# Attention and a feed-forward layer on one core: weight preparation at the lowest rank, x written in one piece, two steps of each block held back

## The chip, the cores and the metric

The kernel runs on one core of a Trainium2 chip. The metric is the device time of one execution in microseconds (us), the median of three runs. The kernel is written against a tile framework: the program is emitted by Python code, and a scheduler sets at build time in which order the instructions stand on each engine.

## The reference

Softmax attention with a learned relative-position bias, followed by a feed-forward layer with a hard-swish-like gate:

```python
scores = (q @ k.transpose(0, 1, 3, 2)) / sqrt(D)          # B=4, H=8, S=576, D=64
x = (log1p(|i - j|) / log1p(max(i, 1)))[..., None]
bias = relu(x @ w1 + b1) @ w2                             # hidden 32, one value per head
attn = softmax(scores + bias)                             # over the keys
y = attn @ v                                              # to [B*S = 2304 tokens, 512]
h = y @ w_in                                              # 512 x 2048
g = h * clip(h + 3, 0, 6) / 6
out = g @ w_out                                           # 2048 x 512
```

The feed-forward weights arrive as 64-bit floats.

## The kernel before

**Units and tiles.** The attention is cut into 32 units (b, p, u): a batch b, one of four pairs of heads p, and a part u of the query rows. Part u=0 has 256 query rows (four tiles t = 0 to 3, each 128 rows of one pair), part u=1 has 320 (five tiles t = 4 to 8; tile 8 holds the last 64 rows of both heads). That makes 144 tiles. The loop over n walks them: `front(n)` issues QK of tile n+1 (PE, `s_ps`, L560 or L540), the softmax's first pass on DVE (`bt`, `sm`, L572), the division into a high and a low fp16 part (`hl`: ACT L129, DVE L146), three tiles later the transposing DMA from SP's queue (`at<-hl`, L648), and at a unit's end PV (PE, `pv_ps`, L719, 28 matmuls). `back(n)` writes x, that is the attention output scaled and split into fp16 high (ACT, L733) and low (DVE, L146) parts, and runs the exponential (ACT, L583). The units with b < 2 and u=0 take a "direct" fp32 path instead (`t_ps`, `atf`, L631, L673).

**Feed-forward blocks.** When all four pairs of a (b, u) are through, its x is a block of 256 or 320 tokens, and `ffn(b, u)` is put on a queue. It is a generator of 32 steps of 12 matmuls: 16 h-steps (`h_ps`, L794, contracting over all 512 columns of x, each followed by ACT, DVE, ACT and POOL work on the result: L784, L777, L771, L773) and 16 o-steps (`o_ps`, L817). The loop takes about 1.55 to 2 such steps for each tile, by a credit. From tile 37 on (`steady`), PE executes in the order in which the code emits: a matmul that must wait holds up everything behind it on PE. Four PSUM banks are shared by `h_ps`, `o_ps`, `pv_ps` and the bias's `b_ps`.

**Weights.** `w_in_prep` and `w_out_prep` (generators `gen_w` and `gen_o`) load each weight in eight pieces, rebuild it on ACT, POOL and DVE (L258 to L272), take its largest value, and bring that to one number over all partitions through a small transpose on PE (`m_ps`, L159; then `p_w` L161 and a row of small DVE instructions that ends in `r_w1c` or `r_w2c`, L222), by which the rows are scaled. `r_w2c` also scales the first block's g (L127), and only then can the first o_ps begin. The scheduler picks among ready instructions by a rank; the generators run through `low`, which shifts the rank by `CFG['pw']` and `CFG['po']` (both 0 before). `CFG['os']` is the number of w_out steps after which they are taken at a faster rate.

The bias tensor is computed on the way (`z_e`, `b_ps`, `bo`), written to memory and read back by tile (`bt<-bias`).

Of the kernel before, what the change touches and what calls it, by code (L numbers as in the profile page):

```python
# [29 lines left out]
CFG = {'z0': 'AD', 'gz': 12, 'z1': 'AD', 'gz2': 16, 'zeng': 'DDA', 'sg': 'P', 'wm1': 'A', 'wm2': 'RRAAAAAA', 'hl': 'A', 'gl': 'PP', 'vm': 'A', 'g0': 8, 'rwi': 2.0, 'rw0': 0.3, 'rw1': 0.7, 'ro': 0.85, 'rb': 1.7, 'rf0': 1.3, 'rf': 2.0, 'rf1': 1.55, 'la': 6, 'gq': 2, 'gap': 0.0, 'wu': 8, 'act': 'o', 'g1': 2, 'w64': 5, 'rfo': 2.3, 'tv': 'A', 'pw': 0, 'po': 0, 'gr': 'AD', 'wb': 3, 'fb': 2, 'spn': 45, 'sw': 37, 'ws': 2, 'kn': 10, 'kw': 1, 'os': 11, 'ro2': 2.0, 'bo': 12, 'rb0': 1.5, 'psw': 21, 'xp': 0, 'mw': 2, 'he': 0}  # L30
# [5 lines left out]
def attention_moe_kernel(  # L36
# [227 lines left out]
    def f64_pack(lo, sign, u, top):  # L264
        ub = u.bitcast(U32)
        nc.vector.tensor_scalar(
            out=u, in0=u, scalar1=F64_MAX, scalar2=0.0, op0=ALU.min, op1=ALU.max, accum_out=top,
        )
        nc.vector.scalar_tensor_tensor(
            out=ub, in0=ub, scalar=3, in1=sign, op0=ALU.logical_shift_left, op1=ALU.bitwise_or  # L270
        )
        nc.vector.scalar_tensor_tensor(  # L272
            out=ub, in0=lo, scalar=29, in1=ub, op0=ALU.logical_shift_right, op1=ALU.bitwise_or
        )
# [9 lines left out]
    def w_in_prep():  # L284
# [19 lines left out]
        def pack(k, tu):  # L304
            f64_pack(*tu, parts[:, k:k + 1])
            if k % 2:
                c = k // 2
                nc.vector.tensor_reduce(
                    out=top[:, c:c + 1], in_=parts[:, k - 1:k + 1], op=ALU.max, axis=AX.X
                )  # L310
                row_scale(top[:, c:c + 1], pw[:, c:c + 1], sw[:, c:c + 1])
# [196 lines left out]
    COLS = [0, 256, 128, 384, 0, 384, 128, 512, 256]  # L508
# [102 lines left out]
    def direct(b, p, t):  # L611
        return b < cfg["fb"] and t < 4

    def unit_tile(n):
# [8 lines left out]
        return at_t[b, p, u][:, :, COLS[t]:COLS[t] + 128]  # L623
# [22 lines left out]
    def soft_turn(n):  # L646
        if not direct(*tiles[n]):
            nc.sync.dma_start_transpose(out=unit_tile(n), in_=a_t.pop(n))  # L648

    XPARTS = [  # L650
        [(slice(0, 128), 0, 256, 0)],
        [
            (slice(0, 64), 0, 320, 0),
            (slice(64, 128), 0, 64, 256),
            (slice(64, 128), 64, 320, 0),
        ],
    ]
# [69 lines left out]
    def x_high(b, p, u):  # L727
        if direct(b, p, 4 * u):
            return x_first(b, p)
        ps = pv_t[b, p, u]  # L730
        x = x_tile(b, u)
        for rows, lo, hi, tok in XPARTS[u]:
            nc.scalar.activation(  # L733
                out=x[rows, 0, p, tok:tok + hi - lo], in_=ps[rows, lo:hi], func=AF.Copy,
                scale=pscale["x"][rows, p:p + 1],
            )

    def x_low(b, p, u):
# [4 lines left out]
        for rows, lo, hi, tok in XPARTS[u]:  # L743
            low_part(
                x[rows, 1, p, tok:tok + hi - lo], ps[rows, lo:hi],
                pscale["x"][rows, p:p + 1], x[rows, 0, p, tok:tok + hi - lo],
            )
# [398 lines left out]
    START, SWITCH = 21, cfg["sw"]  # L1146
    in_order = ctx.enter_context(ExitStack())
# [46 lines left out]
    out_steps = [0]  # L1194

# [6 lines left out]
    def ffn_step():  # L1202
        nonlocal phase
        r = next(queue[0], "end")
        if r == "w2":
            phase = 1.5
        if r == "end":
            queue.pop(0)
            phase = 2
# [10 lines left out]
    for n in range(-1, NT + 7):  # L1220
# [22 lines left out]
        if queue:  # L1243
# [4 lines left out]
            while credit >= 1.0 and queue and (phase < 2 or steady[0] or cfg["he"]):  # L1248
# [69 lines left out]
```

## Time and profile before

| | us |
|---|---|
| median of 3 runs | 681.77 (680.17 to 683.64) |
| the profiled execution | 680.92 |
| its span | 679.1 |
| PE busy | 631.2 |
| ACT busy | 519.8 |
| DVE busy | 478.9 |

The profiled execution is read from its first to its last instruction (the span). The execution's own time has 1.8 us around the span. A busy time is the sum of the stretches in which an engine had an instruction under way, not the time at which it works at its peak.

### The profile page before, as it was taken

Reading aid. Unit: us, or ns where it says so; the run is one execution under the profiler, and the core shown is the slowest. Engines: PE = TensorE matmul, PEld = TensorE weight load, DVE = VectorE, ACT = ScalarE, POOL = GpSimd, SP = SyncE. Lnnn points to the kernel's source line nnn. Section 1 sums busy time; section 2 is a strip of 40 time slices with the busy share of each in tenths; the row PEclk is TensorE's granted clock in tenths of the full one; section 3 lists DMA queues with packets and bytes.
Section 4 is the critical chain, followed back from the end, with each engine's and each line's share of the span. In section 5 each row is a group of like instructions: output and inputs, shape, how many; then the busy total and the mean of one; then the engine's idle time right before and its main releaser. Section 6 shows DMA issues by size and latency. Waiting matters only on the chain. (4 is left out here: it accounts for less than half of the span.)

```text
span 679.1 us, 14803 instructions
## 1 busy us (share of the span) xinstructions
PE 631.2 (93%) x5424; PEld 449.8 (66%) x5424; DVE 478.9 (71%) x1150; ACT 519.8 (77%) x1032; POOL 210.6 (31%) x267
## 2 busy tenths in 40 slices
PE   7677889787998999999999999999999999999997
PEld 2224546555676767688887786767776777777775
DVE  7889977999737887777688777777777768811310
ACT  7986877887939997998699878987799779922620
POOL 1111115855102441154134413541244313310420
PEclk9997999997999999999999999999999999999999
DMA  8899768571768979979999899979977796420000
GB/s 295 297 339 339 296 246 317 184 271 57 192 182 208 236 191 283 217 217 203 280 278 232 175 202 195 190 148 181 206 178 150 166 197 126 98 60 20 1 11 29
DMA packets 176136, 130.56 MB, mean 192 GB/s; under 512 B 137792, under 2 KB 145216, under 8 KB 175040
## 3 DMA queue, kind: packets, MB, share of 16 engines
q1 hardware_dynamic: 166272, 114.14, 67.5%
q10 hardware_dynamic: 9792, 15.49, 7.1%
q8 instruction: 42, 0.69, 0.4%
q14 instruction: 30, 0.25, 0.1%
HBM read 77.54 MB, written 15.49 MB: 137 GB/s over the span
## 5 line engine op out<-in xcount | busy, mean ns | idle before, releaser
L794 PE MATMUL h_ps<-x,wi 128*128 128x256 f16 (+1 forms) x1536 | 199.7, 287 | 8.3 <-DVE t L777 4.0
L817 PE MATMUL o_ps<-g,wo 128*128 128x256 f16 (+1 forms) x1536 | 195.8, 286 | 0.3 <-DVE t L777 0.3
L794 PEld LDWEIGHTS <-wi 128*128 128x128 f16 x1536 | 147.2, 98 | 56.5 <-issue 14.4
L817 PEld LDWEIGHTS <-wo 128*128 128x128 f16 x1536 | 147.0, 98 | 47.0 <-issue 10.0
L773 POOL TENSOR_TENSOR g<-t,g 128x256 f16<-128x256 f32 (+1 forms) x128 | 101.6, 805 | 165.1 <-ACT g L771 155.4
L583 ACT ACTIVATE bt<-bt,sm 128x576 f32<-128x576 f32 x144 | 110.6, 769 | 43.6 <-DVE sm L572 41.2
L146 DVE SCALAR_TENSOR_TENSOR hl<-bt,sm,hl 128x576 f16<-128x576 f32 x112 | 93.9, 854 | 25.1 <-ACT hl L129 22.4
L419 POOL TENSOR_TENSOR qkl<-st,qkh 128x576 fp32r<-128x576 f32 (+2 forms) x48 | 56.4, 1196 | 98.3 <-ACT qkh L412 98.2
L129 ACT ACTIVATE hl<-bt,sm 128x576 f16<-128x576 f32 x112 | 83.9, 768 | 2.8 <-ACT bt L583 1.4
L777 DVE SCALAR_TENSOR_TENSOR t<-t,t,h_ps 128x320 f32<-128x320 f32 (+1 forms) x112 | 56.4, 515 | 37.0 <-ACT t L784 35.3
L572 DVE CUSTOM_DVE_ANT_0 bt<-s_ps,bt 128x576 f32<-128x576 f32 x88 | 64.7, 750 | 12.2 <-PE s_ps L560 5.7
L784 ACT ACTIVATE t<-h_ps,t,hr 128x320 f32<-128x320 f32 (+1 forms) x112 | 64.5, 588 | 4.4 <-PE h_ps L794 3.3
L771 ACT ACTIVATE g<-t 128x256 f16<-128x256 f32 (+1 forms) x128 | 55.0, 440 | 15.5 <-DVE t L777 14.8
L827 ACT ACTIVATE ot<-o_ps,os 128x256 f32<-128x256 f32 (+1 forms) x32 | 15.9, 496 | 52.7 <-PE o_ps L817 52.6
L591 DVE TENSOR_SCALAR sm<-sm 128x1 f32<-128x1 f32 x112 | 16.9, 151 | 42.9 <-ACT bt L583 42.7
L869 DVE TENSOR_SCALAR z_e<-T,nbp 128x576 f32<-128x576 f32 (+17 forms) x69 | 36.0, 568 | 4.3 <-PE b_ps L890 4.2
L929 ACT ACTIVATE bo<-b_ps,cv_sb,isc 128x576 f32<-128x576 f32 (+36 forms) x60 | 35.8, 636 | 2.5 <-PE b_ps L890 2.5
L146 DVE SCALAR_TENSOR_TENSOR x<-pv_ps,xr,x 64x320 f16<-64x320 f32 (+3 forms) x56 | 23.6, 445 | 18.1 <-ACT x L733 17.0
L873 ACT ACTIVATE z_e<-T,bp 128x576 f32<-128x576 f32 (+17 forms) x43 | 28.9, 694 | 9.7 <-PE b_ps L890 4.3
L631 PE MATMUL t_ps<-eye_sb,bt 128*128 128x128 f32 x160 | 26.3, 299 | 10.6 <-DVE sm L572 5.7
L631 PEld LDWEIGHTS t_ps<-eye_sb,bt 128*128 128x128 f32 x160 | 18.8, 150 | 20.9 <-ACT atf L634 7.8
L719 PE MATMUL pv_ps<-at,vh 128*64 128x320 f16 (+1 forms) x432 | 32.0, 293 | 0.3 <-DVE t L777 0.3
(127 smaller groups left out, 860.4 us busy)
## 6 DMA issues: line engine op xcount, KB each, us to landing
bt<-bias SPq DMA_DIRECT2D x36, 576.0 KB, 5.0
w<-in_w_in_dram SPq DMA_DIRECT2D x8, 1024.0 KB, 7.2
vs<-in_vp_dram SPq DMA_DIRECT2D x24, 320.0 KB, 4.4
st<-in_qk_dram SPq DMA_DIRECT2D x16, 448.0 KB, 4.6
bias<-bo ACTq DMA_DIRECT2D x20, 295.5 KB, 4.5
wo<-in_w_out_dram SPq DMA_DIRECT2D x5, 1024.0 KB, 5.9
bias<-bo ACTq DMA_DIRECT2D x16, 288.0 KB, 6.3
bt<-bias SPq DMA_DIRECT2D x32, 144.0 KB, 3.2
```

The costliest lines, as they stand in the source:

```text
L129: nc.scalar.activation(out=out, in_=full, func=AF.Copy, scale=scale)
L146: nc.vector.scalar_tensor_tensor(out=out, in0=full, scalar=scale, in1=high, op0=ALU.mult, op1=ALU.subtract)
L419: nc.gpsimd.tensor_sub(out=lo[:, c:c + w], in0=t[:, c:c + w], in1=hi[:, c:c + w].bitcast(F32))
L572: nc.vector.tensor_tensor_reduce(out=halves(bt), in0=ps, in1=halves(src), op0=ALU.add, op1=ALU.min, scale=-0.125, scalar=3.0e38, accum_out ...
L583: nc.scalar.activation(out=bt, in_=bt, func=AF.Exp, scale=-1.0, bias=sm[:, 0:1], accum_out=total)
L631: nc.tensor.transpose(tp[:, 128 * c:128 * c + 128], bt[:, j:j + 128], eye_sb)
L771: nc.scalar.activation(out=g[:, 0], in_=uu, func=AF.Copy)
L773: e.tensor_sub(out=g[:, 1], in0=uu, in1=g[:, 0])
L777: nc.vector.scalar_tensor_tensor(out=t_t[f], in0=t_t[f], scalar=cols(f)[2], in1=h_t.pop(f)[:, 0:n], op0=ALU.min, op1=ALU.mult,)
L784: nc.scalar.activation(out=t_t[f], in_=h_t[f][:, 0:n], func=AF.Relu, scale=cols(f)[0], bias=cols(f)[1],)
L794: nc.tensor.matmul(out=h_t[f][:, 0:n], lhsT=wi[:, a, c, f * 128:(f + 1) * 128], rhs=x[:, e, c], start=(k == 0), stop=(k == 3 * KC - 1),)
L817: nc.tensor.matmul(out=ops[:, 0:n], lhsT=wo[:, a, f, e * 128:(e + 1) * 128], rhs=g_t[f][:, r], start=(f == 0 and a == 0 and r == 0), stop= ...
```

## The change

In the table `CFG`, `pw` and `po` go from 0 to 1000, so that weight preparation ranks behind every other ready instruction, and `os` goes from 11 to 10. The rest is in the code:

- The packing of w_in chains its maximum through the accumulator's starting value instead of reducing two partial maxima (four small DVE instructions fewer).
- Tiles 5 and 7 go to other columns of the unit's transposed tile, and tile 8's transposing DMA is split into two of 64 rows, so that the columns of both heads' tokens lie together. x of a 320-token unit is then one 128x320 piece on ACT and one on DVE, where it was three each (64x320, 64x64, 64x256).
- In `steady`, when only one block is on the queue and 30 of its 32 steps are taken, its last two steps are kept back until the next block is queued (`held`), up to tile 149 (`LAST`). A block is queued one tile after PV of its last pair was issued and its x written.

```diff
@@ -261,10 +261,10 @@
         )
         return lo, hi.bitcast(U32), u
 
-    def f64_pack(lo, sign, u, top):
+    def f64_pack(lo, sign, u, top, first=0.0):
         ub = u.bitcast(U32)
         nc.vector.tensor_scalar(
-            out=u, in0=u, scalar1=F64_MAX, scalar2=0.0, op0=ALU.min, op1=ALU.max, accum_out=top,
+            out=u, in0=u, scalar1=F64_MAX, scalar2=first, op0=ALU.min, op1=ALU.max, accum_out=top,
         )
         nc.vector.scalar_tensor_tensor(
             out=ub, in0=ub, scalar=3, in1=sign, op0=ALU.logical_shift_left, op1=ALU.bitwise_or
@@ -302,12 +302,11 @@
             return f64_abs(t, stage[:, c, fs])
 
         def pack(k, tu):
-            f64_pack(*tu, parts[:, k:k + 1])
-            if k % 2:
-                c = k // 2
-                nc.vector.tensor_reduce(
-                    out=top[:, c:c + 1], in_=parts[:, k - 1:k + 1], op=ALU.max, axis=AX.X
-                )
+            c = k // 2
+            if k % 2 == 0:
+                f64_pack(*tu, parts[:, c:c + 1])
+            else:
+                f64_pack(*tu, top[:, c:c + 1], parts[:, c:c + 1])
                 row_scale(top[:, c:c + 1], pw[:, c:c + 1], sw[:, c:c + 1])
 
         def split(k, step):
@@ -505,7 +504,7 @@
         return out, src
 
     ORDER = [(0, 0), (0, 1), (1, 0), (1, 1), (2, 0), (2, 1), (3, 0), (3, 1), (4, 0)]
-    COLS = [0, 256, 128, 384, 0, 384, 128, 512, 256]
+    COLS = [0, 256, 128, 384, 0, 320, 128, 448, 256]
     UT = (range(4), range(4, 9))
     units = [(b, p, u) for u in range(2) for b in range(B) for p in range(PAIRS)]
     tiles = [(0, p, t) for ts in ((0, 1), (2, 3)) for p in range(2) for t in ts]
...
@@ -644,17 +647,16 @@
         a_t[n] = hl
 
     def soft_turn(n):
-        if not direct(*tiles[n]):
-            nc.sync.dma_start_transpose(out=unit_tile(n), in_=a_t.pop(n))
-
-    XPARTS = [
-        [(slice(0, 128), 0, 256, 0)],
-        [
-            (slice(0, 64), 0, 320, 0),
-            (slice(64, 128), 0, 64, 256),
-            (slice(64, 128), 64, 320, 0),
-        ],
-    ]
+        if direct(*tiles[n]):
+            return
+        hl = a_t.pop(n)
+        if tiles[n][2] < 8:
+            nc.sync.dma_start_transpose(out=unit_tile(n), in_=hl)
+            return
+        at = whole_unit(n)
+        for s in range(2):
+            c = 256 + QW[1] * s
+            nc.sync.dma_start_transpose(out=at[:, :, c:c + 64], in_=hl[64 * s:64 * s + 64])
 
     def x_tile(b, u):
         if (b, u) not in x_t:
@@ -729,22 +731,16 @@
             return x_first(b, p)
         ps = pv_t[b, p, u]
         x = x_tile(b, u)
-        for rows, lo, hi, tok in XPARTS[u]:
-            nc.scalar.activation(
-                out=x[rows, 0, p, tok:tok + hi - lo], in_=ps[rows, lo:hi], func=AF.Copy,
-                scale=pscale["x"][rows, p:p + 1],
-            )
+        nc.scalar.activation(
+            out=x[:, 0, p], in_=ps[:, 0:QW[u]], func=AF.Copy, scale=pscale["x"][:, p:p + 1]
+        )
 
     def x_low(b, p, u):
         if direct(b, p, 4 * u):
             return
         ps = pv_t.pop((b, p, u))
         x = x_tile(b, u)
-        for rows, lo, hi, tok in XPARTS[u]:
-            low_part(
-                x[rows, 1, p, tok:tok + hi - lo], ps[rows, lo:hi],
-                pscale["x"][rows, p:p + 1], x[rows, 0, p, tok:tok + hi - lo],
-            )
+        low_part(x[:, 1, p], ps[:, 0:QW[u]], pscale["x"][:, p:p + 1], x[:, 0, p])
 
     def ffn(b, u):
         x = x_t.pop((b, u))
@@ -1144,6 +1140,7 @@
     credit = 0.0
     out_ready = False
     START, SWITCH = 21, cfg["sw"]
+    HOLD, LAST = 2, NT + 5
     in_order = ctx.enter_context(ExitStack())
 
     def keep_order(*names):
@@ -1192,6 +1189,10 @@
         keep_order("PE")
 
     out_steps = [0]
+    taken = [0]
+
+    def held():
+        return steady[0] and len(queue) == 1 and n < LAST and taken[0] >= 32 - HOLD
 
     def out_step():
         if next(gen_o, "end") == "end":
@@ -1201,11 +1202,13 @@
 
     def ffn_step():
         nonlocal phase
+        taken[0] += 1
         r = next(queue[0], "end")
         if r == "w2":
             phase = 1.5
         if r == "end":
             queue.pop(0)
+            taken[0] = 0
             phase = 2
         return r != "end" and r != "w2"
 
@@ -1245,7 +1248,7 @@
                 credit = cfg["gap"]
             else:
                 credit += cfg["rf0"] if phase == 1 else cfg["rfo"] if phase < 2 else cfg["rf1" if unit_no[min(n, NT - 1)] >= 16 else "rf"]
-            while credit >= 1.0 and queue and (phase < 2 or steady[0] or cfg["he"]):
+            while credit >= 1.0 and queue and (phase < 2 or steady[0] or cfg["he"]) and not held():
                 if ffn_step():
                     credit -= 1.0
                 if phase == 1.5 and not out_ready:
```

What the change moves, as the scheduler puts it.

SP's queue at the start of the program, before (`w` are pieces of w_in, `qk` and `vf` operands of the direct path):

```order
L248 DMA w_181<-in_w_in_dram 128x2048
L248 DMA w_185<-in_w_in_dram 128x2048
L395 DMA qk_219<-in_qkd_dram 128x1088
L395 DMA qk_237<-in_qkd_dram 128x1088
L395 DMA qk_255<-in_qkd_dram 128x1088
L395 DMA qk_280<-in_qkd_dram 128x1088
L179 DMA vf<-in_vp_dram 128x640
L248 DMA w_262<-in_w_in_dram 128x2048
```

The same place after the change:

```order
L394 DMA qk_219<-in_qkd_dram 128x1088
L394 DMA qk_237<-in_qkd_dram 128x1088
L394 DMA qk_255<-in_qkd_dram 128x1088
L394 DMA qk_280<-in_qkd_dram 128x1088
L179 DMA vf<-in_vp_dram 128x640
L248 DMA w_181<-in_w_in_dram 128x2048
L248 DMA w_185<-in_w_in_dram 128x2048
L248 DMA w_262<-in_w_in_dram 128x2048
```

The first two pieces of w_in moved behind the five loads of the direct path.

DVE at the second weight reduction, from the reduced maximum `p_w` to `r_w2c`, before:

```order
L146 SCALAR_TENSOR_TENSOR wo<-cu,w2s,wo 128x1024
L161 TENSOR_REDUCE p_w_1698<-m_ps 128x1
L146 SCALAR_TENSOR_TENSOR hl<-bt,sm,hl 128x576
L220 RECIPROCAL rm_w_1700<-p_w_1698 128x1
L203 TENSOR_SCALAR os_1761<-hs_992,p_w_1698 128x1
L203 TENSOR_SCALAR os_2157<-hs_2153,p_w_1698 128x1
L203 TENSOR_SCALAR os_3351<-hs_3347,p_w_1698 128x1
L146 SCALAR_TENSOR_TENSOR hl<-bt,sm,hl 128x576
L222 TENSOR_SCALAR r_w2c<-w2p,rm_w_1700 128x8
```

And after the change:

```order
L152 TENSOR_REDUCE m_w_1690<-w2p 128x1
L594 RECIPROCAL sm<-sm 128x1 x2
L161 TENSOR_REDUCE p_w_1694<-m_ps 128x1
L203 TENSOR_SCALAR os_1770<-hs_988,p_w_1694 128x1
L203 TENSOR_SCALAR os_2166<-hs_2162,p_w_1694 128x1
L220 RECIPROCAL rm_w_1696<-p_w_1694 128x1
L203 TENSOR_SCALAR os_3366<-hs_3362,p_w_1694 128x1
L222 TENSOR_SCALAR r_w2c<-w2p,rm_w_1696 128x8
L146 SCALAR_TENSOR_TENSOR wo<-cu,w2s,wo 128x1024
```

The two `hl` (softmax's low parts) that stood between `p_w` and `r_w2c` stand behind it now, with seven of the g scalings ahead of them.

PE just ahead of the first o_ps, before (`s_ps` is QK, `t_ps` the direct path's transposes, the twelve h_ps matmuls of one step end in the first row here):

```order
L794 MATMUL h_ps<-x,wi 128x256
L560 MATMUL s_ps<-qkh 128x288 x2
L560 MATMUL s_ps<-qkl,qkh 128x288 x2
L560 MATMUL s_ps<-qkh,qkl 128x288 x2
L631 MATMUL t_ps<-eye_sb,bt 128x128 x5
L817 LDWEIGHTS wo
L817 MATMUL o_ps<-g,wo 128x256
L817 LDWEIGHTS wo
L817 MATMUL o_ps<-g,wo 128x256
L817 LDWEIGHTS wo
L817 MATMUL o_ps<-g,wo 128x256
```

And after the change, first the rows ahead of the same twelve h_ps (they begin in the last row):

```order
L634 MATMUL t_ps<-eye_sb,bt 128x128 x10
L559 MATMUL s_ps<-qkh 128x288 x2
L559 MATMUL s_ps<-qkl,qkh 128x288 x2
L559 MATMUL s_ps<-qkh,qkl 128x288 x2
L559 MATMUL s_ps<-qkh 128x288 x2
L559 MATMUL s_ps<-qkl,qkh 128x288 x2
L559 MATMUL s_ps<-qkh,qkl 128x288 x2
L159 MATMUL m_ps<-eye_sb,m_w_1690 128x128
L790 LDWEIGHTS wi
L790 MATMUL h_ps<-x,wi 128x256
```

then the rows behind them:

```order
L790 MATMUL h_ps<-x,wi 128x256
L886 MATMUL b_ps<-z_e,w_sb 32x320 x4
L813 LDWEIGHTS wo
L813 MATMUL o_ps<-g,wo 128x256
L813 LDWEIGHTS wo
L813 MATMUL o_ps<-g,wo 128x256
```

One more tile's three `s_ps` groups and the five `t_ps` used to stand between these h_ps and the first o_ps. The `s_ps` groups moved ahead of `m_ps`, the `t_ps` behind 45 of the o_ps matmuls. In the blocks from tile 37 on, PE's list after the change is one or two steps (12 or 24 matmuls) further along in each block than before. Where a block ends, PE's list had 36 o_ps matmuls of the old block behind the last pair's PV and now has 24, at the PV that ends at 337.84 us in the profile and at the one that ends at 401.62 us; right behind the 24 come h_ps matmuls of the new block.

## Rows read from the trace of the kernel before

**Rows 1.** The page: busy time by engine, and the chain that ended last, by line.

```profile
PE 631.2 (93%) x5424; PEld 449.8 (66%) x5424; DVE 478.9 (71%) x1150; ACT 519.8 (77%) x1032; POOL 210.6 (31%) x267
...
PE o_ps L817 16%; PE h_ps L794 12%; PE s_ps L560 3%; PE pv_ps L719 3%; DVE hl L146 1%; ACT hl L129 0%; ACT bt L583 0%; DVE x L146 0%; ACT t L784 0%; DMA bt<-bias 0%; DVE bt L572 0%; SPq L498 0%; ACT ot L827 0%; DVE t L777 0%; ACT vh L129 0%
```

**Rows 2.** Busy time by stage: start:end, length, busy us (instructions), PE clock, DMA share, GB/s.

```profile
0.00:160.00 160.00, 129.37 (x961) 72.27 (x961) 141.80 (x304) 129.49 (x218) 56.26 (x51) 0.98 0.76 276
160.00:172.50 12.50, 9.19 (x41) 6.93 (x42) 11.82 (x38) 7.86 (x15) 1.73 (x4) 0.59 0.35 85
172.50:205.00 32.50, 32.50 (x290) 23.85 (x288) 16.11 (x47) 21.46 (x44) 3.60 (x5) 1.00 0.71 192
205.00:245.00 40.00, 35.56 (x355) 25.88 (x354) 32.88 (x86) 39.04 (x85) 15.94 (x22) 1.00 0.86 200
245.00:515.00 270.00, 263.90 (x2495) 204.93 (x2493) 203.23 (x505) 230.37 (x487) 93.26 (x133) 1.00 0.96 212
```

**Rows 3.** Timeline of PE, 162 to 174 us: start, us, instruction, count, [idle before <-releaser].

```profile
162.52 1.33 PE L631 MATMUL t_ps<-eye_sb,bt 128*128 128x128 f32 x5 [3.87 <-DVE sm L572]
...
167.64 0.80 PE L159 MATMUL m_ps<-eye_sb,m_w 128*128 128x128 f32 x2
168.23 2.77 PE L794 MATMUL h_ps<-x,wi 128*128 128x256 f16 x12
...
172.56 0.49 PE L817 MATMUL o_ps<-g,wo 128*128 128x256 f16 x3
```

**Rows 4.** Timeline of DVE around the second p_w.

```profile
168.47 0.29 DVE L161 TENSOR_REDUCE p_w<-m_ps 128x1 f32<-128x128 f32 x1 [0.47 <-PE m_ps L159]
168.68 0.81 DVE L146 SCALAR_TENSOR_TENSOR hl<-bt,sm,hl 128x576 f16<-128x576 f32 x1
...
170.56 0.23 DVE L222 TENSOR_SCALAR r_w2c<-w2p,rm_w 128x8 f32<-128x8 f32 x1
```

**Rows 5.** Line 794: its matmuls, with first and last start; DVE's first p_w.

```profile
L794 PE MATMUL h_ps<-x,wi x1536: 269/299/422, 107.5 to 649.3; 128*128 128x256 f16 x96, 128*128 128x320 f16 x96
...
86.33 0.29 DVE L161 TENSOR_REDUCE p_w<-m_ps 128x1 f32<-128x128 f32 x1
```

**Rows 6.** Tile x: counts, duration ns min/median/max, span of starts, forms.

```profile
L733 ACT ACTIVATE x<-pv_ps,xr x56: 308/456/522, 220.4 to 612.8; 64x320 f16<-64x320 f32 x16, 64x64 f16<-64x64 f32 x16, 64x256 f16<-64x256 f32 x16, 128x256 f16<-128x256 f32 x8
L146 DVE SCALAR_TENSOR_TENSOR x<-pv_ps,xr,x x56: 290/486/545, 221.6 to 614.0; 64x320 f16<-64x320 f32 x16, 64x64 f16<-64x64 f32 x16, 64x256 f16<-64x256 f32 x16, 128x256 f16<-128x256 f32 x8
```

**Rows 7.** Timeline of DVE and PE at one x in three pieces.

```profile
356.62 1.25 DVE L146 SCALAR_TENSOR_TENSOR x<-pv_ps,xr,x 64x320 f16<-64x320 f32 x3
...
357.92 1.26 PE L794 MATMUL h_ps<-x,wi 128*128 128x256 f16 x10 [0.80 <-DVE x L146]
```

**Rows 8.** Waits of PE: us in total, times, longest.

```profile
PE h_ps L794 <- DVE x L146: 3.2, 4, 0.9
```

**Rows 9.** Timeline of PE and DVE where a block ends, 128x256 x.

```profile
337.84 4.10 PE L817 MATMUL o_ps<-g,wo 128*128 128x256 f16 x36
...
340.47 0.48 DVE L146 SCALAR_TENSOR_TENSOR x<-pv_ps,xr,x 128x256 f16<-128x256 f32 x1
```

**Rows 10.** The next block's end, 128x320 x: PE, then ACT, then DVE.

```profile
401.62 4.11 PE L817 MATMUL o_ps<-g,wo 128*128 128x256 f16 x36
...
405.18 1.19 ACT L733 ACTIVATE x<-pv_ps,xr 64x320 f16<-64x320 f32 x3
...
405.45 0.81 DVE L146 SCALAR_TENSOR_TENSOR hl<-bt,sm,hl 128x576 f16<-128x576 f32 x1
406.40 1.25 DVE L146 SCALAR_TENSOR_TENSOR x<-pv_ps,xr,x 64x320 f16<-64x320 f32 x3
```

**Rows 11.** SP: the transposes (count, ns min/median/max, starts), and its waits.

```profile
L648 SPq DMA_TRANSPOSE at<-hl x112: 1242/1332/2941, 169.5 to 597.5; - x112
...
DMA to landing us min/median/max: 3.2/4.4/8.8
...
SPq L648 <- DVE hl L146: 48.7, 26, 7.6
```

More of the change, by code (lines that the diff above doesn't have):

```diff
@@ L29 @@
 VC = 5 * 128
-CFG = {'z0': 'AD', 'gz': 12, 'z1': 'AD', 'gz2': 16, 'zeng': 'DDA', 'sg': 'P', 'wm1': 'A', 'wm2': 'RRAAAAAA', 'hl': 'A', 'gl': 'PP', 'vm': 'A', 'g0': 8, 'rwi': 2.0, 'rw0': 0.3, 'rw1': 0.7, 'ro': 0.85, 'rb': 1.7, 'rf0': 1.3, 'rf': 2.0, 'rf1': 1.55, 'la': 6, 'gq': 2, 'gap': 0.0, 'wu': 8, 'act': 'o', 'g1': 2, 'w64': 5, 'rfo': 2.3, 'tv': 'A', 'pw': 0, 'po': 0, 'gr': 'AD', 'wb': 3, 'fb': 2, 'spn': 45, 'sw': 37, 'ws': 2, 'kn': 10, 'kw': 1, 'os': 11, 'ro2': 2.0, 'bo': 12, 'rb0': 1.5, 'psw': 21, 'xp': 0, 'mw': 2, 'he': 0}
+CFG = {'z0': 'AD', 'gz': 12, 'z1': 'AD', 'gz2': 16, 'zeng': 'DDA', 'sg': 'P', 'wm1': 'A', 'wm2': 'RRAAAAAA', 'hl': 'A', 'gl': 'PP', 'vm': 'A', 'g0': 8, 'rwi': 2.0, 'rw0': 0.3, 'rw1': 0.7, 'ro': 0.85, 'rb': 1.7, 'rf0': 1.3, 'rf': 2.0, 'rf1': 1.55, 'la': 6, 'gq': 2, 'gap': 0.0, 'wu': 8, 'act': 'o', 'g1': 2, 'w64': 5, 'rfo': 2.3, 'tv': 'A', 'pw': 1000, 'po': 1000, 'gr': 'AD', 'wb': 3, 'fb': 2, 'spn': 45, 'sw': 37, 'ws': 2, 'kn': 10, 'kw': 1, 'os': 10, 'ro2': 2.0, 'bo': 12, 'rb0': 1.5, 'psw': 21, 'xp': 0, 'mw': 2, 'he': 0}
 F64_BIAS = 2.0 ** -112
@@ L612, in direct, with whole_unit @@
         return b < cfg["fb"] and t < 4
-    def unit_tile(n):
+    def whole_unit(n):
         b, p, t = tiles[n]
@@ L622, in unit_tile @@
             at_t[b, p, u] = at
-        return at_t[b, p, u][:, :, COLS[t]:COLS[t] + 128]
+        return at_t[b, p, u]
+    def unit_tile(n):
+        c = COLS[tiles[n][2]]
+        return whole_unit(n)[:, :, c:c + 128]
     def soft_low(n):
```

## The prediction

> **What bounds the kernel now.** I read the page first: PE is busy 631.2 of the span's 679.1 us, and the chain that ended last runs mostly through o_ps, h_ps, s_ps and pv_ps on PE [rows 1]. So only time in which PE stands idle, or runs at its lower clock, can be won; the change removes no matmul. The view by stages says where that time is [rows 2]. In the first 160 us PE is busy 129.4, so 30.6 idle, and DVE is the fullest engine (141.8). From 160 to 172.5 PE is idle 3.3 us more, and the granted clock is 0.59 of full speed there (between the two levels, 1.2 and 2.4 GHz). From 172.5 to 205 PE never stops, while ACT is busy only 21.5 of 32.5 us; from 205 to 245 it is the reverse: ACT 39.0 of 40, PE idle 4.4. From 245 to 515 PE is idle 6.1 of 270 us. Behind that nothing of note is left. So there are three pots: the front (about 34 us, held by DVE and loads), the stretch after the first o_ps (4.4), and the steady stretch (6.1).
>
> Next I read the timelines at the edge between the first two. PE waits 3.87 us for DVE's softmax, does the transposes at half speed, then m_ps, then one h-step of 12 matmuls in 2.77 us, then s_ps and t_ps, and only at 172.56 the first o_ps [rows 3]. At full clock 12 such matmuls take 12 x 4.11/36 = 1.37 us (the 36 at 401.62, of the same shape [rows 10]). DVE has p_w at 168.47 and r_w2c at 170.56 to 170.79, with hl between them [rows 4]. In the steady stretch the waits that the change touches are the four of h_ps for x, 3.2 us together, the longest 0.9 [rows 8]: the new h_ps needs the PSUM bank that the last piece of x has just been read from [rows 7].
>
> **The change part by part.** The sum is made against the profiled execution, 680.92 us, which is 0.85 below the median of 681.77 and inside the runs' spread; I add the same 0.85 at the end.
>
> *Front: rank, reductions, loads.* (a) From p_w to the end of r_w2c takes 170.79 - 168.47 = 2.3 us on DVE; without the two hl of 0.81 [rows 4] it takes 0.7: 1.6 us earlier. (b) On PE, from the end of m_ps's work the h-step (2.77), then s_ps and t_ps, stand ahead of the first o_ps: 172.56 - 167.64 = 4.9 us [rows 3]. Afterwards it is m_ps, h-step, b_ps, o_ps: with 0.4 for b_ps's four rows (an estimate, the size of the three o_ps matmuls at 172.56) and the h-step still at half speed 0.6 + 2.8 + 0.4 = 3.8, so 1.1 less; at full speed 2.4, so 2.5 less. PE and DVE chains lie beside each other, so (a) and (b) do not add: I take 1.6 for both. (c) Four small reductions less on DVE, each shorter than the reduction of 128 columns, 0.29 us [rows 4]: I take 0.1 each, 0.4. (d) Softmax now goes ahead of weight preparation, and what PE waits for longest here is softmax (3.87 [rows 3]). The work on DVE is the same, so most of this comes back; I take 1.0 of the 3.87, with 0 and 3.9 as ends. (e) The first loads of w_in leave behind five others, and each piece is prepared some places later. That is a loss only if the h-steps wait for it: the first reduction is over at 86.33 and the first h_ps runs at 107.5 [rows 5], 21 us later, so I cost it at nothing. Without that cover every microsecond would pass on; the upper end is 2 us. Together -3.0, between -6 and +2.
>
> *QK ahead of the first long o stretch.* One more tile's s_ps stands ahead of the o_ps. With it the two softmaxes, exponentials and hl that follow can run while ACT idles 11.0 us between 172.5 and 205 [rows 2], instead of queuing in 205 to 245 where ACT is full and PE loses 4.4. Two tiles of ACT work are 2 x 2 pieces of some 0.8 us (hl on DVE takes 0.81 [rows 4], ACT's share is similar in size): about 3 us of ACT work moved from a full stretch into an empty one. PE can win at most the 4.4; I take 2.5, with ends 0 and 3.4.
>
> *x in one piece.* Three pieces take 1.25 us on DVE [rows 7], 1.19 on ACT [rows 10]. The longest single piece of any form took 0.545 and 0.522 us [rows 6], and a 128x320 piece has as many columns as the longest of them (64x320); so 0.55 and 0.52. Each of the sixteen units gains 0.7 on both engines, but only the four waits turn that into PE time: 4 x 0.7 = 2.8, capped by the wait that is shorter than 0.7, so 2.7. The ends are 1.0 (if another instruction on DVE is what is late next) and 3.2 (all of the wait).
>
> *The split transposes.* Sixteen more DMAs on SP's queue. A transpose's issue takes 1.33 us there by the median [rows 11], so at most 16 x 1.33 = 21.3 us more on SP, and nothing if two halves cost as much as a whole. SP stood idle 48.7 us for hl alone ahead of transposes, in 26 waits [rows 11], so there is room, and what is queued behind (loads of q, k, v and bias, the next transposes) has had it too. Cost 0, upper end 1.3 (one issue exposed once). One rule speaks against it. The Trainium skill, "DMA: Bandwidth & Descriptors", section "Anatomy of one DMA", puts a fixed cost of about 2.0 us, mostly completion, on every DMA beside its bytes (fitted on another issuing path): sixteen more would be 32 us if they stood one behind another. The trace has 3.2 to 8.8 us from issue to landing [rows 11], which holds such a share, but two halves can be under way together.
>
> *The two steps held back.* PE executes in the written order, so what stands between the last pair's PV and the first h_ps of the new block is the only cover for writing x. That was 36 o_ps matmuls and further work; it is now 24 in two places. 24 x 4.11/36 = 2.74 us. PV's end is read from the start of the o_ps right behind it. At the first place, PV ends at 337.84 and the low part of x at 340.47 + 0.48 = 340.95, 3.1 later [rows 9]: PE is short by 0.4. At the second, PV ends at 401.62; ACT began x at 405.18, three pieces [rows 10]. In one piece it ends at 405.70; DVE's hl is over at 406.26, and x's low part ends at 406.8: 5.2 behind PV, so PE is short by 5.2 - 2.7 = 2.5. Behind the waiting h_ps stand QK of the next tile and, through it, softmax on DVE and ACT. At the other block ends the list keeps 36 or more. Together +2.9, with 0 (ACT and DVE come to x sooner, since the tiles ahead of it were earlier) and +6 (both late, and the QK behind it late for softmax) as ends.
>
> *The sum:* -3.0 - 2.5 - 2.7 + 0 + 2.9 = -5.3. 680.92 - 5.3 = 675.6 on the profiled scale, 676.5 on that of the median.
>
> **The rivals.** *First, the front gives nothing and only the steady stretch moves.* The work of DVE in the first 160 us is the same but for some tenths, and DVE is busy 141.8 of it [rows 2]. If preparation ends as late as before because it is now behind everything, (a) to (d) cancel: -2.5 - 2.7 + 2.9 = -2.3, so 679.5. For it: the amount of work; against it: the places on DVE between p_w and r_w2c, which changed for certain.
> *Second, the front gives more.* If softmax ahead of preparation takes away all of the 3.87 us wait, and the clock does not fall (the fall follows PE's idle time here), the front gives 6, the o stretch 3.4 and x its 3.2, with 2.9 lost: 681.77 - 9.7 = 672.
> *Third, the other side: the hold.* PE comes to the ends of blocks with only 24 matmuls in hand, and x is late. It decides from the point where the shortage at a block's end passes about 3 us: with ACT and DVE as full as between 205 and 245, x would come 6 us behind PV at five block ends, 5 x (6 - 2.7) = +16 against -8.2 of gains: 690. For it speaks that x came 5.2 us behind PV by the working above at one end; against it that the list shows 24 at two ends only. With those two alone (+6.6) the gains still win.
> *Fourth, preparation too late.* If the first h_ps, which has 21 us of cover, or the first o_ps, which has none, is reached later because preparation starves, the end moves by as much. From 8 us of delay on the gains are gone; at 12 it is 686.
> *Fifth, the transposes lie on the path:* +21.3 - 5.3, 698. Each PV would then show a wait for a transpose; there is none among PE's waits today that I count on, so little speaks for it. By the page's 2.0 us it would be 708.
>
> **How the numbers follow.** A change of 0.5% (3.4 us, about what a measurement of this kernel can tell from no change) puts the bounds at 678.4 and 685.2. Chances: my forecast (673 to 679) 0.45; the front gives nothing 0.22; the front gives more 0.13; the hold 0.08; preparation late 0.10; transposes 0.02. Faster: 0.40 of the forecast, all of the second rival, and 0.04 of the first, 0.57. Slower: about 0.07 of the hold, 0.06 of late preparation, 0.02: 0.15. The same: the rest, 0.28. The range, with no more than 2 in 10 outside, goes from 669 (most of the upper ends of the gains) to 684 (first rival, and the milder half of the third and fourth). The likeliest case's own range is 673 to 679.
>
> **What would show it right or wrong.** Right: the first o_ps starts near 169.6 instead of 172.56; r_w2c follows p_w within 1 us; PE is idle some 2 us between the first o_ps and the 75 us behind it, not 4.4; the four waits of h_ps for x shrink to near zero, and in their place two waits for x of 0.4 and 2.5 us stand at the block ends near 340 and 400; x is one instruction of about 0.52 us on ACT and 0.55 on DVE. Wrong: the first h_ps is later than 107.5 by more than its cover, or the first o_ps is not earlier than 172; PE shows waits for x of several us at three or more block ends; or pv_ps waits for a transposing DMA.

## The result, and the profile after

The changed kernel takes 670.36 us in the median of four runs (669.22 to 673.99), the kernel before 680.97 on the same chip: a ratio of 0.9849, with a 95% interval of 0.9813 to 0.9884, so 7.9 to 12.7 us less. The forecast was 676.5, from 669 to 684. The profiled execution of the changed kernel is the longest of its four: its span is 672.2 us, 6.9 less than the 679.1 of before.

The page: busy time, and the chain that ended last, by line, to be held against [rows 1].

```profile
PE 634.2 (94%) x5424; PEld 452.4 (67%) x5424; DVE 460.0 (68%) x1114; ACT 506.4 (75%) x1000; POOL 207.6 (31%) x267
...
PE o_ps L813 16%; PE h_ps L790 16%; PE s_ps L559 4%; PE pv_ps L721 4%; ACT vh L129 0%; DVE x L146 0%; ACT ot L823 0%; DVE hl L146 0%; DVE vl L146 0%; DVEq L146 0%
```

The busy time by stage, with the same bounds and columns as [rows 2]:

```profile
0.00:160.00 160.00, 131.31 (x950) 73.58 (x950) 134.88 (x296) 127.02 (x216) 50.78 (x50) 0.94 0.76 275
160.00:172.50 12.50, 9.54 (x50) 7.54 (x48) 11.42 (x31) 8.94 (x16) 6.42 (x7) 0.64 0.21 61
172.50:205.00 32.50, 32.50 (x270) 22.66 (x269) 20.07 (x61) 23.24 (x48) 3.85 (x6) 0.98 0.83 191
205.00:245.00 40.00, 37.97 (x378) 27.98 (x375) 31.74 (x80) 38.20 (x82) 11.85 (x17) 1.00 0.91 205
245.00:515.00 270.00, 269.17 (x2548) 209.60 (x2547) 198.01 (x495) 227.06 (x478) 97.51 (x140) 1.00 1.02 215
```

From 245 to 515 us PE stood idle 6.1 us before and 0.8 now; from 205 to 245 it was 4.4 and is 2.0. The first two rows hardly moved. So the time came out of the steady stretch, and in this execution the front gave nothing. The front's timeline of PE says the same (compare [rows 3]):

```profile
169.55 0.79 PE L159 MATMUL m_ps<-eye_sb,m_w 128*128 128x128 f32 x2
170.13 2.77 PE L790 MATMUL h_ps<-x,wi 128*128 128x256 f16 x12
172.83 1.20 PE L886 MATMUL b_ps<-z_e,w_sb 128*32 128x320 f32 x8
173.96 1.27 PE L813 MATMUL o_ps<-g,wo 128*128 128x256 f16 x10
```

The first o_ps stands at 173.96, where the forecast had 169.6 and the kernel before 172.56. The way from m_ps to it became shorter (4.4 us against 4.9), but by less than the 1.1 to 2.5 us that were forecast: the b_ps ahead of the o_ps, priced at 0.4, took 1.1 (172.83 to 173.96). And m_ps itself came at 169.55, not 167.64. DVE's part (compare [rows 4]):

```profile
170.38 0.29 DVE L161 TENSOR_REDUCE p_w<-m_ps 128x1 f32<-128x128 f32 x1 [1.04 <-PE m_ps L159]
...
171.14 0.92 DVE L222 TENSOR_SCALAR r_w2c<-w2p,rm_w 128x8 f32<-128x8 f32 x1
```

No hl stands between p_w and r_w2c any more, as the order said, but r_w2c itself took 0.92 us, where it took 0.23 before [rows 4]. It ends 1.7 us behind p_w's start, against 2.3 before and the 0.7 of the forecast. The first h_ps came 5 us later than before [rows 5]:

```profile
L790 PE MATMUL h_ps<-x,wi x1536: 269/299/422, 112.4 to 642.3; 128*128 128x256 f16 x96, 128*128 128x320 f16 x96
```

x is one instruction per pair, as long as forecast (compare [rows 6]), and the waits of h_ps for it went from 3.2 us [rows 8] to 0.4:

```profile
L734 ACT ACTIVATE x<-pv_ps,xr x24: 452/505/527, 223.2 to 608.3; 128x320 f16<-128x320 f32 x16, 128x256 f16<-128x256 f32 x8
L146 DVE SCALAR_TENSOR_TENSOR x<-pv_ps,xr,x x24: 464/538/551, 225.4 to 608.9; 128x320 f16<-128x320 f32 x16, 128x256 f16<-128x256 f32 x8
...
PE h_ps L790 <- DVE x L146: 0.4, 2, 0.2
```

This is the second of the two block ends, where the forecast had a wait of 2.5 us (compare [rows 10]), PE first, then ACT and DVE:

```profile
400.40 2.79 PE L813 MATMUL o_ps<-g,wo 128*128 128x256 f16 x24
403.03 1.52 PE L790 MATMUL h_ps<-x,wi 128*128 128x320 f16 x10
404.75 0.43 PE L790 MATMUL h_ps<-x,wi 128*128 128x320 f16 x2 [0.19 <-DVE x L146]
...
403.10 0.51 ACT L734 ACTIVATE x<-pv_ps,xr 128x320 f16<-128x320 f32 x1
...
404.15 0.54 DVE L146 SCALAR_TENSOR_TENSOR x<-pv_ps,xr,x 128x320 f16<-128x320 f32 x1
```

PE ran ten of the twelve matmuls of the new block's first h-step before it waited, and then for 0.19 us. The cover is not only the 24 o_ps: an h-step goes through the four pairs one after the other, and only its last three matmuls read the last pair, the first of them x's high part alone. And x's low part ended at 404.69, 4.3 us behind the end of PV, where the forecast had 5.2. So of the 2.5 us some 0.9 went because x came sooner and some 1.4 because the ten h_ps cover too. At the first block end PE did not wait for x.

### The profile page after: what moved, and what is told of

Read it like the earlier page. It is cut to its first block, busy times and chain, and to the rows that moved or that the text cites. A ratio compares the mean times of both kernels' runs of the same rounds, so it can differ in the third digit from the quotient of the medians.

```text
span 672.2 us, 14784 instructions
## 1 busy us (share of the span) xinstructions
PE 634.2 (94%) x5424; PEld 452.4 (67%) x5424; DVE 460.0 (68%) x1114; ACT 506.4 (75%) x1000; POOL 207.6 (31%) x267
## 5 line engine op out<-in xcount | busy, mean ns | idle before, releaser
L418 POOL TENSOR_TENSOR qkl<-st,qkh 128x576 fp32r<-128x576 f32 (+2 forms) x48 | 54.8, 1163 | 67.7 <-ACT qkh L411 67.0
L865 DVE TENSOR_SCALAR z_e<-T,nbp 128x576 f32<-128x576 f32 (+17 forms) x69 | 31.4, 500 | 7.7 <-PE b_ps L886 6.6
L571 DVE CUSTOM_DVE_ANT_0 bt<-s_ps,k 128x576 f32<-128x576 f32 x40 | 28.7, 752 | 9.6 <-PE s_ps L559 7.6
```

Source lines behind the costliest of these rows:

```text
L418: nc.gpsimd.tensor_sub(out=lo[:, c:c + w], in0=t[:, c:c + w], in1=hi[:, c:c + w].bitcast(F32))
L571: nc.vector.tensor_tensor_reduce(out=halves(bt), in0=ps, in1=halves(src), op0=ALU.add, op1=ALU.min, scale=-0.125, scalar=3.0e38, accum_out ...
```

## The experiments

Each run was timed in five rounds beside the kernel before on the same chip, and has a profile. Since PE's list is fixed from tile 37 on, the profile can be read by two landmarks on PE: the start of the first pv_ps of the transposed path (PV 1 below) and that of the last (PV 24). Up to PV 1 is the front, the weights and the direct path; between them lies the steady stretch; behind PV 24 only feed-forward work is left. These are the two landmarks in the timeline of the kernel before, then in that of the changed kernel:

```profile
216.47 1.17 PE L719 MATMUL pv_ps<-at,vh 128*64 128x256 f16 x18
...
609.88 1.42 PE L719 MATMUL pv_ps<-at,vh 128*64 128x320 f16 x18
```

```profile
219.63 1.18 PE L721 MATMUL pv_ps<-at,vh 128*64 128x256 f16 x18
...
606.16 1.41 PE L721 MATMUL pv_ps<-at,vh 128*64 128x320 f16 x18
```

In the table, "between" is PV 24 less PV 1, "behind" the span less PV 24, both from the profile; the ratio is that of the timed runs.

| run | PV 1 | between | behind | span | ratio to before, 95% interval |
|---|---|---|---|---|---|
| before | 216.5 | 393.4 | 69.3 | 679.1 | |
| changed | 219.6 | 386.5 | 66.0 | 672.2 | 0.9849 (0.9813 to 0.9884) |
| e1 rank, chained maximum, os | 217.2 | 388.9 | 69.3 | 675.3 | 0.9947 (0.9924 to 0.9969) |
| e2 x alone | 215.0 | 388.3 | 69.3 | 672.6 | 0.9912 (0.9887 to 0.9936) |
| e3 hold alone | 213.9 | 397.4 | 66.0 | 677.3 | 1.0005 (0.9986 to 1.0025) |
| e4 changed, ranks 0, os 11 | 222.0 | 389.5 | 66.0 | 677.6 | 0.9955 (0.9935 to 0.9975) |
| e5 changed, no hold | 218.0 | 383.8 | 69.3 | 671.0 | 0.9892 (0.9868 to 0.9916) |
| e6 changed, x in pieces | 216.5 | 393.9 | 66.0 | 676.4 | 0.9975 (0.9958 to 0.9992) |
| e7 changed, two steps ahead, no hold | 217.6 | 388.7 | 66.0 | 672.4 | 0.9880 (0.9853 to 0.9906) |
| e8 changed, no chained maximum | 216.5 | 386.4 | 66.0 | 668.9 | 0.9907 (0.9877 to 0.9936) |
| e9 os alone | 218.4 | 389.0 | 69.3 | 676.6 | 0.9961 (0.9947 to 0.9975) |
| e10 rank and chained maximum, os 11 | 214.0 | 393.1 | 69.3 | 676.3 | 0.9991 (0.9973 to 1.0009) |
| e11 x's high part in one piece | 214.4 | 390.7 | 69.3 | 674.3 | 0.9965 (0.9945 to 0.9985) |
| e12 x and os alone | 218.2 | 383.8 | 69.2 | 671.3 | 0.9876 (0.9858 to 0.9895) |

Between the two landmarks PE stood idle 9.6 us in the kernel before and 2.3 in the changed one; it was 5.1 in e2, 7.4 in e9 and 2.9 in e12.

**e1, the first part alone.** The kernel before with `pw`, `po` at 1000, `os` at 10 and the chained maximum:

```diff
-'pw': 0, 'po': 0, ... 'os': 11
+'pw': 1000, 'po': 1000, ... 'os': 10
```

> The rank of weight preparation, the chained maximum and the faster w_out steps after ten, on the kernel before; x in three pieces, no hold. By the prediction (front -3.0, o stretch -2.5): 5.5 us faster than before, first o_ps near 169.6 us. By the rival that the profile of the changed kernel suggests (the front gives nothing, since first o_ps came at 174.0 there against 172.56): within 2 us of before.

It is 2.1 to 5.2 us faster. The first o_ps stands at 171.4 and PV 1 at 217.2: no shorter front. The gain, 4.5 us, lies between the PVs.

**e2, x alone.** The columns, the split transposing DMA and the one piece of x, on the kernel before:

```diff
-        for rows, lo, hi, tok in XPARTS[u]:
-            nc.scalar.activation(
-                out=x[rows, 0, p, tok:tok + hi - lo], in_=ps[rows, lo:hi], func=AF.Copy,
...
+        nc.scalar.activation(
+            out=x[:, 0, p], in_=ps[:, 0:QW[u]], func=AF.Copy, scale=pscale["x"][:, p:p + 1]
+        )
...
```

> x in one piece and tile 8's transposing DMA in two, alone, on the kernel before. By the prediction: 2.7 us faster, the four waits of h_ps for x (3.2 us) shrink to 0.5 and no pv_ps waits for a transpose. By the rival that transposes cost: slower by up to 21 us. By the rival that another DVE instruction is late next: under 1 us faster.

4.4 to 7.7 us faster, 5.1 of it between the PVs: about double the forecast. No wait for x is left on PE, and something else fell with it. PE's waits of before for the softmax's first pass, and those of e2:

```profile
PE s_ps L560 <- DVE sm L572: 1.9, 2, 1.2
```

```profile
PE s_ps L560 <- DVE sm L572: 0.4, 1, 0.4
```

Softmax work stands behind the three pieces too, on ACT and on DVE, and QK waited for the bank that softmax had yet to read: 0.73 and 1.21 us at 398.60 and 415.35 in the kernel before. (e11 tells the two engines apart.) 3.2 for x and 1.5 of these make 4.7 of the 5.1. No pv_ps waited for a transposing DMA.

**e3, the hold alone.** On the kernel before, `held` as in the change:

```diff
...
+        return steady[0] and len(queue) == 1 and n < LAST and taken[0] >= 32 - HOLD
...
```

> The two steps held back, alone, on the kernel before, with x in three pieces. By the prediction: slower, by 2.9 us and more, since three pieces of x are later still (0.7): h_ps waits at two block ends. By the rival: the queue never runs empty, so the credit goes on accruing, each block runs one or two steps further ahead, 24 o_ps matmuls (2.7 us) leave the end of the program and fill idle time of PE in the steady stretch: 2.5 to 5 us faster.

No difference in time. Between the PVs it is 4.0 us longer, behind them 3.3 shorter. Two of its waits on PE, one for g and one for x at the second block end:

```profile
378.32 0.27 PE L817 MATMUL o_ps<-g,wo 128*128 128x256 f16 x1 [1.73 <-ACT g L771]
...
407.93 0.43 PE L794 MATMUL h_ps<-x,wi 128*128 128x320 f16 x2 [0.79 <-DVE x L146]
```

With x in three pieces the wait at this end is 0.8 us, again behind ten h_ps matmuls; it is not the 2.5 and more that the forecast worked out. The 3.3 us behind PV 24 are two steps of 12 matmuls that were taken earlier: its list has 60 o_ps matmuls of the old block there, before it was 84. They cost no less where they now stand: of the 4.0 us more between the PVs, 3.7 are busy time of PE. A part of that is a lower clock: the granted clock was 0.50 from 380.0 to 383.4 us, right behind the waits for g. So the rival was right about the moving and wrong about idle time that they would fill.

**e4, the changed kernel without the rank.**

```diff
-'pw': 1000, 'po': 1000, ... 'os': 10
+'pw': 0, 'po': 0, ... 'os': 11
```

> The changed kernel with the ranks back at 0 and os at 11; x in one piece, hold and the chained maximum stay. By the prediction: about 5 us slower than the changed kernel, so 675 to 676, or by its own terms the same as before (-2.7 + 2.9). By the rival (the gain lies in the steady stretch): the gain is kept but for 0 to 3 us, so 670 to 674.

678.29 us, 2.6 less than before. Neither expectation holds: the front became worse, with the first o_ps at 181.4 and PV 1 at 222.0. PE waits 8.94 us in one place for softmax, while DVE works through weight preparation; its timeline over the same time:

```profile
172.71 1.33 PE L634 MATMUL t_ps<-eye_sb,bt 128*128 128x128 f32 x5 [8.94 <-DVE sm L571]
```

```profile
163.27 2.11 DVE L272 SCALAR_TENSOR_TENSOR cu<-wo,cu 128x1024 uint32<-128x1024 uint32 x1
...
167.90 2.41 DVE L269 SCALAR_TENSOR_TENSOR cu<-cu,z_e 128x1024 uint32<-128x1024 uint32 x1
...
171.90 0.74 DVE L571 CUSTOM_DVE_ANT_0 bt<-s_ps,k 128x576 f32<-128x576 f32 x1
```

Of what sets it apart from e2 and e3, whose PV 1 stands at 215.0 and 213.9, only the chained maximum acts so early. So an order without the rank can be much worse. That these few reductions decide whether the scheduler meets it is argued, not shown: the chained maximum at rank 0 was not run by itself on the kernel before.

**e5, the changed kernel without the hold.**

```diff
-            while credit >= 1.0 and queue and (phase < 2 or steady[0] or cfg["he"]) and not held():
+            while credit >= 1.0 and queue and (phase < 2 or steady[0] or cfg["he"]):
```

> The changed kernel without the hold; rank, chained maximum and x in one piece stay. By the prediction, in which the hold costs 2.9 us: 667.5. By the single runs added up (rank -3.8, x -5.2): about 672, so the hold is worth 1 to 2 us once x is in one piece. By hold alone, which moved nothing: 670.

673.23 us. Its interval overlaps that of the changed kernel, so the timed runs don't settle whether the hold is worth 1 or 2 us. The landmarks: without the hold 2.8 us less between the PVs, 3.3 more behind them, 0.5 in all.

**e6, the changed kernel with x in pieces**, the edit of e2 undone.

> The changed kernel with x in three pieces, the old columns and one transposing DMA for tile 8; rank and hold stay. By the prediction: 2.7 us slower than the changed kernel, 673. By x alone (-5.2): 675 to 676. By the rival that the hold needs the short x (with three pieces the wait at block ends and for g showed 1.7 and 1.1 us in hold alone): more than the 5.2, so 677 to 678, no better than rank alone.

678.61 us, 0.25% less than before; between the PVs 7.4 us more than the changed kernel. That is more than the 5.1 that x is worth without the hold, as the rival had it. PE's idle time there is 5.6 us more and its busy time 1.8 more. The busy time is again a lower clock: 0.60 from 379.0 to 382.4 us, behind a wait of 1.74 us for g as in e3; no run with x in one piece has that wait. So what the hold adds to the cost of late pieces is mostly this stretch; each of the two runs has one profile.

**e7, two steps ahead without the hold.**

```diff
-            while credit >= 1.0 and queue and (phase < 2 or steady[0] or cfg["he"]) and not held():
+            if n == 53:
+                credit += 2.0
+            while credit >= 1.0 and queue and (phase < 2 or steady[0] or cfg["he"]):
```

> The changed kernel without the hold, but with two steps of credit given once at tile 53, so that PE's list runs two steps ahead as with the hold, and differs from it only where one block ends (12 o_ps matmuls behind PV instead of 24). If what the hold brings is running two steps ahead: as the changed kernel, within 1 us, with one wait for x of about 1 us near 340. If it is the cover of x at block ends: about 2 us slower. By the prediction (cover short by 2.9 in two places, more with 12 matmuls): 4 us slower than without the hold.

672.45 us, the same as the changed kernel within the intervals. Between the PVs it has 2.2 us more, but 1.7 of this is one stretch of 48 h_ps matmuls at a lower clock (7.07 us, and 5.40 in e5). At the block end with only 12 o_ps behind PV it waited 0.17 and 0.25 us for x. So, by these profiles, running ahead is nearly all that the hold brings here, and its cover of x is worth half a microsecond.

**e8, the four small reductions back** in the changed kernel.

```diff
+            f64_pack(*tu, parts[:, k:k + 1])
+            if k % 2:
+                c = k // 2
+                nc.vector.tensor_reduce(
...
```

> The changed kernel with the four small reductions of the w_in maxima back. By the prediction 0.4 us slower, which is inside the noise: 670 to 671. By the rival that these four instructions alter the order of the front (the run with ranks at 0 and the chained maximum had its first o_ps at 181.4): 2 us or more either way.

674.86 us in the median, from 670.88 to 675.75, against 670.36 for the changed kernel; the two intervals overlap only at their ends (0.9877 and 0.9884). Its profiled execution, the fastest of its six, has the shortest span of all the profiles, with 386.4 between the PVs, as the changed kernel. So between the PVs the chained maximum does nothing with the rank in place; whether it is worth some us in the front, as the medians would have it, stays open.

**e9, one number.** `os` from 11 to 10 on the kernel before.

> The kernel before with one number changed: the faster w_out steps begin after 10 steps instead of 11. By the prediction (this number was given no term): as before, 680 to 681. By the theory from the traces so far, that it starts the bias a tile earlier and so moves its last group out of the stretch behind the first blocks: from the first to the last PV some 4.5 us shorter, 2 to 4.5 us faster in all.

1.7 to 3.6 us faster, and the same 4.4 us less between the PVs as e1. 2.7 us of it are in one place. The kernel before has two groups of the bias's b_ps between the first h-steps of a block, here the second of them:

```profile
284.36 2.10 PE L890 MATMUL b_ps<-z_e,w_sb 128*32 128x512 f32 x16
287.10 1.14 PE L794 MATMUL h_ps<-x,wi 128*128 128x256 f16 x9 [0.64 <-DVE t L777]
```

The same place in e9, where the bias began one tile earlier and the second group has left:

```profile
280.77 1.18 PE L890 MATMUL b_ps<-z_e,w_sb 128*32 128x512 f32 x16
281.88 5.41 PE L794 MATMUL h_ps<-x,wi 128*128 128x256 f16 x48
```

The group held PE for 2.1 us, where the one that stands here in e9 takes 1.2, and the h_ps behind it waited 0.64 more. Most of the rest lies ahead of 250 us, where PE's waits behind PV 1 fell from 3.5 us to 2.0. Each group stands earlier now, and one more of them, the one of 128x384, is done ahead of PV 1. PV 1 in turn comes later: 218.4 and 218.2 in the two runs with `os` at 10 and rank 0 (e9, e12), against 216.5 in the kernel before, all three with a granted clock of 0.59 from 160 to 172.5 us.

**e10, rank and chained maximum without os.** As e1, with `os` at 11.

> Rank and chained maximum alone, with os left at 11; x in three pieces, no hold. By the prediction (all of it from the rank): 675 to 676. By the theory that os brought the gain: no faster than before, first o_ps near 171 to 174, and from the first to the last PV within 1 us of before; the front 0 to 2 us longer.

No difference: 0.9973 to 1.0009. Between the PVs 0.3 us less. PV 1 at 214.0 lies in the spread of the runs with the front of before. The rank by itself gives nothing that these runs can tell, although softmax and QK moved ahead. Two more pairs differ in rank and chained maximum alone and say the same: e1 against e9 (0.9947 and 0.9961) and e5 against e12 (0.9892 and 0.9876), with 388.9 and 389.0 and twice 383.8 us between the PVs.

**e11, which of the two pieces.** The new columns and transposes, x's high part (ACT) in one piece, the low part (DVE) in three:

```diff
-        low_part(x[:, 1, p], ps[:, 0:QW[u]], pscale["x"][:, p:p + 1], x[:, 0, p])
+        for rows, lo, hi in ([(slice(0, 128), 0, 256)], [(slice(0, 64), 0, 320), (slice(64, 128), 0, 64), (slice(64, 128), 64, 320)])[u]:
+            low_part(x[rows, 1, p, lo:hi], ps[rows, lo:hi], pscale["x"][rows, p:p + 1], x[rows, 0, p, lo:hi])
```

> On the kernel before: new columns and split transposing DMA, x's high part in one piece on ACT, its low part still in three on DVE. If DVE's pieces are what made both x and the softmax behind them late: the gain from the first to the last PV falls from 5.1 us to below 1, the waits of h_ps for x come back (3 us) and those of s_ps for sm (1.9 us). If ACT's pieces counted: half or more of the 5.1 stays. If the split transposes cost anything it shows here as slower than before.

2.7 of the 5.1 us stay, so ACT's pieces counted as much as DVE's. PE's waits for softmax's first pass, and one of its waits for x:

```profile
PE s_ps L560 <- DVE sm L572: 0.3, 1, 0.3
```

```profile
439.18 2.08 PE L792 MATMUL h_ps<-x,wi 128*128 128x320 f16 x14 [0.30 <-DVE x L146]
```

With DVE's three pieces kept, QK's waits for softmax fell all the same, from 1.9 us to 0.3. So it was not DVE's pieces that made softmax late; by this run it was ACT's (the new columns and the split transposes, which are in it too, were not run apart). Around the four places where h_ps waited for x before, 3.2 us together, it still waits 2.8: twice 0.30 for x, as above, and 0.79 and 1.39 us for ACT's and DVE's work on h. In e2, with one piece on DVE too, h_ps has no wait there. So most of the gain on these waits needs DVE's one piece.

The split transposes are in this kernel too, and it is faster than before. SP's rows for the split DMAs in the changed kernel:

```profile
L659 SPq DMA_TRANSPOSE at<-hl x32: 1199/1276/2670, 339.3 to 594.3; - x32
```

An issue of 64 rows takes 1.28 us on SP, one of 128 rows took 1.33 [rows 11]. So the split does cost SP nearly its full upper bound, some 16 x 1.28 = 20 us of 21, and no instruction of PE waits for it.

**e12, x and os alone**, without rank, chained maximum and hold.

> The kernel before with only x in one piece and os at 10: no rank, no chained maximum, no hold. If rank and hold bring nothing: from the first to the last PV 9.6 us shorter than before, and 669 to 672, as fast as the changed kernel or 1 to 2 us faster by its shorter front. By the prediction (rank gives the front): 5 us slower than the changed kernel less the hold's 2.9, so 673 or more.

672.3 us, 0.9858 to 0.9895: as fast as the changed kernel within the intervals. The terms add up: 4.4 for os and 5.1 for x make 9.5, and 9.6 were measured between the PVs. No version ran measurably faster than the changed kernel.

## Why the prediction was right or wrong

The direction and the range hold; the gain was twice the forecast of 5.3 us, by terms that were off in both directions.

*The front, -3.0: wrong in size, and hardly to be seen.* (a) and (b) went the way that the order showed, at half of their size or less: r_w2c's end came 0.6 us closer to p_w, not 1.6, and from m_ps to the first o_ps it is 0.5 less, not 1.1 and more. But the forecast set one execution, whose first o_ps stood at 172.56, against a time worked out. Seen over all runs, the first o_ps stands between 170.0 and 172.6 us in the four with the old front (before, e2, e3, e11) and between 170.2 and 174.0 in those with rank and `os`.

At a like granted clock from 160 to 172.5 us, 0.59 or 0.60, it stands at 171.4, 172.2, 170.7 and 171.8 with the rank (e1, e5, e6, e7) and at 172.6, 173.6 and 173.5 without it (before, e9, e12); at 0.73 it is 170.2 and 169.8 (e8, e10) against 171.1 and 170.5 (e2, e11). So the rank brings 1 to 2 us there. m_ps does not come earlier by it (166.6 to 168.2 in the four, 167.1 to 167.6 in the three, at the like clock), so (c) and (d) brought nothing that can be seen. A likely reason, not shown by itself, is that another tile's QK now stands ahead of m_ps: the prediction counted only what had left the place behind m_ps, and that is work moved, not removed. By PV 1 about 1 us is left (216.5 to 218.0 in e1, e5, e6 and e7 against 218.4 and 218.2 in e9 and e12), and e10 (0.9991) gives nothing that the timed runs can tell. So the rival "the front gives nothing" is nearer to it than the forecast. One of the prediction's signs of being wrong, a first o_ps not earlier than 172, was there in the changed kernel's profile (173.96). (e) held: the first h_ps came 5 us later in the changed kernel and 3 us later in e10, whose PV 1 is no later, so the 21 us of cover were cover.

*QK ahead of the o stretch, -2.5: the size was met by luck, the cause is another.* PE's idle time from 205 to 245 did fall by 2.4 us, from 4.4 to 2.0. But with the rank and `os` at 11 (e10) it is 3.4, with `os` alone (e9) 2.2; and between the PVs e10 gains 0.3 us and e9 4.4. It is `os`, to which the prediction gave no term: the bias's groups stand earlier, and one leaves the block at 284 us. Of the 4.4 us some 2 are paid back ahead of PV 1; 2.8 us are left in the timed runs of e9.

*x in one piece, -2.7: right in mechanism, too small.* It measured 5.1 between the PVs. The prediction capped the term at h_ps's waits for x and left out that softmax work stands behind the same pieces, on ACT above all (e11), so that QK's waits (1.9 us, 0.4 left) fell as well.

*The split transposes, 0: right*, and by the reason given: SP has the room, at nearly the full price of the issues.

*The hold, +2.9: wrong twice.* The step "24 x 4.11/36 = 2.74 us of cover" failed: nine more h_ps matmuls do not read the last pair, and the tenth reads its high part only, so they cover too; and x was there 0.9 us sooner than worked out. At the two block ends PE waited 0 and 0.19 us for x, not 0.4 and 2.5. And the sum left out what follows from the order for the program's end: 24 matmuls less behind the last PV (3.3 us), which stand between the PVs now (2.8). Net -0.5 by the landmarks.

Put together for the two profiled executions: 6.9 us less between the PVs, 3.3 less behind them, 3.2 more up to PV 1. That the median gained 10.6 where this pair of profiles shows 6.9 lies, as far as the profiles tell, in the front: this execution of the changed kernel was its slowest, and e8, with the same 386.4 between the PVs, has PV 1 3.2 us earlier. What of the front's 219.6 is the execution and what is the change stays open within these 3 us.

So the time fell into the range partly by luck. The two terms for the rank, -5.5 together, brought about 1 us, and the hold's +2.9 did not come; the gain is x at twice its price and `os`, which had none. The likeliest case's own range, 673 to 679, was missed. The second rival's 672 is the nearest number, but its mechanism, a front that gives 6 us, did not happen.

## What to carry to other kernels

When an engine executes in a fixed order, read what a wait really needs before pricing its cover: a matmul group that walks through its operand reads the late part last. A long instruction on an engine, or three short ones in its place, delays everything queued behind it, so list all who wait for that engine, not only who waits for that tile. And when a change moves work without removing it, count both ends: what a stretch takes on, another stretch gives up.

## What the runs showed of the hardware

The kernel before, e2, e3 and e11 have word for word the same order on PE up to the first o_ps, and PV 1 at 216.5, 215.0, 213.9 and 214.4. From 160 to 172.5 us the granted clock was 0.59 of full speed in the kernel before [rows 2] and 1.00 in e3, here with the columns of [rows 2]:

```profile
160.00:172.50 12.50, 8.33 (x63) 5.98 (x63) 12.18 (x44) 11.30 (x22) 3.04 (x5) 1.00 0.52 116
```

The first o_ps came at 172.56 in the one and at 170.0 in the other. e2 and e11 lie between them in the clock (0.73), in the first o_ps (171.1 and 170.5) and in PV 1. In the kernel before, the half-speed transposes follow a wait of 3.87 us [rows 3]. So a few microseconds of the front differ from one execution to the next, and in these four they go with the level of the clock; that is as much as a part of this change is worth. The stretch between the PVs repeats within about 0.1 us in kernels that differ in the front alone (388.9 and 389.0 in e1 and e9, 383.8 in e5 and e12), but for the runs in which the clock fell there too (e3 and e6 near 380 us, e7 near 228).
